# Block-sparse attention and a rational feed-forward layer on one core: turning x by DMA instead of by TensorE, and stores issued by ScalarE

## The chip, the cores and the metric

The kernel runs on one core of a Trainium2 chip. The metric is the device time of one execution in microseconds. Three executions of the kernel before took 824.51, 824.73 and 821.61 us; the median is 824.51 us.

The core has a matrix engine (TensorE, "PE" in the profile, with its weight loads as "PEld"), VectorE ("DVE"), ScalarE ("ACT"), GpSimd ("POOL") and SyncE ("SP"). Each runs its own list of instructions in order. DMAs are issued by one of these engines and then run beside them; a DMA that must wait for a semaphore holds up everything that stands behind it in the list of the engine that issues it.

## The reference

```python
# q, k, v: (4, 8, 768, 64); 24 blocks of 32; 3 sampled key blocks for each query block
scores = scale * np.matmul(q, k.transpose(0, 1, 3, 2))
mask = np.abs(blk_i - blk_j) <= 1
mask = mask | (blk_i == 0) | (blk_j == 0) | (blk_i == n_blocks - 1) | (blk_j == n_blocks - 1)
for qb in range(n_blocks):
    for kb in sampled_blocks[qb]:
        mask[qb * block:(qb + 1) * block, kb * block:(kb + 1) * block] = True
scores = np.where(mask, scores, -1000000000.0)
attn = np.exp(scores - np.max(scores, axis=-1, keepdims=True))
attn = attn / (np.sum(attn, axis=-1, keepdims=True) + 1e-09)
x = np.matmul(attn, v).transpose(0, 2, 1, 3).reshape(3072, 512)

h = x @ w_in                                     # (3072, 2048)
P = a[0] + a[1] * h + a[2] * h * h + a[3] * h * h * h
Q = 1.0 + np.abs(b[0]) * np.abs(h) + np.abs(b[1]) * h * h
out = (P / (Q + 1e-06)) @ w_out                  # (3072, 512)
```

## The kernel before

The 3072 tokens are four batches of 768. A batch has 24 query blocks, worked in pairs (`attention`), and three chunks of 256 tokens, so there are 12 chunks `c` in all. The feed-forward layer runs in units `(c, u)`, eight to a chunk, each with 256 of the 2048 hidden columns (`unit`): the products with w_in into the PSUM tile `ph`, an elementwise chain over ScalarE and VectorE, and the products with w_out into `acc`. A unit needs x of its whole chunk, with features on the partitions, as a high and a low fp16 part (`xh`, `xl`).

Attention makes x with tokens on the partitions: scores from the turned keys `kg` (or `kall`) and queries, row maxima, exponentials, the turning of the probabilities, the products with gathered values `vg` into `av`, and a multiplication by the reciprocal row sum into `xn` (`weigh`, line 983). Four blocks share one `xn`, of which there is one buffer; two such groups make a chunk. A group is then turned by four fp32 transposes on TensorE into one of three shared PSUM banks (`turn_x`, line 995), and two instructions take it out of PSUM, scaled by a power of two, as the high and the low part: `evac_high` on ScalarE (recorded under line 150) and `evac_low` on VectorE (line 1006).

The keys of a batch are turned on TensorE and, for batches 1 to 3, stored to a DRAM scratch `ks` by SP (line 604), from where the key blocks of each part are fetched: a run of four neighbours (line 794), the two edge blocks when a buffer is new to the batch (line 797), and six sampled rows (line 801), whose numbers SP loads into registers (line 717). The pair of the first and the last block of a batch attends to everything and takes three parts of eight blocks (lines 792 and 926). Value blocks come straight from the input (lines 926 to 936) into four `vg` buffers, two for each of a pair's blocks. Output rows are copied from `acc` on ScalarE into an `ld` buffer and stored by SP (line 1159). Nearly all DMAs of the kernel stand in SP's list.

The order of the instructions is made when the kernel is built. Every step is an `Op` with an engine, a price in nanoseconds, its predecessors, a priority and the buffers that it takes; `issue` (line 172) goes through the ops that are ready and always takes the one that can start earliest by these prices, ties by priority. The result is a fixed list for each engine. A price that is a list describes DMAs: each holds the issuing engine for its first number, and the transfer follows. Buffers are tickets of a `Ring`. A pool `ext` opens only when the last weights have been decoded (`switch`, line 1223); it gives four more `ld` buffers and two more key buffers.

Of the kernel before, what the change touches and what calls it, by code (L numbers as in the profile page):

```python
# [24 lines left out]
def kernel(  # L25
# [27 lines left out]
    nc = tc.nc  # L53
# [44 lines left out]
    LAT = {(SC, TE): 410, (VE, TE): 240, (PO, TE): 225, (TE, SC): 200, (TE, VE): 200, (TE, SY): 170, (VE, SC): 130, (VE, PO): 130,  # L98
           (SC, VE): 155, (SC, PO): 180, (PO, VE): 80, (PO, SC): 100}
    OWN = {VE: 127, SC: 143, PO: 96}  # L100
    MARGIN, LATE = 17.0, 1500.0

    class Ring:

# [28 lines left out]
    def row(eng, steps, after, prio, takes=(), uses=()):  # L133

        o, after = None, list(after)
        for n, (price, run) in enumerate(steps):
            o = Op(eng, price, run, [o] if n else after, prio, takes=() if n else takes, uses=list(uses) + (list(takes) if n else []))
        return o
# [144 lines left out]
    r_pr, r_st, r_pT, r_av = Ring([None] * 3), Ring([None] * 4), Ring([None] * PT), Ring(range(2))  # L283
    r_ld, r_kt = Ring([p3] * 3), Ring([p1])
    r_ldq, r_qt, r_fc, r_ks = Ring([None]), Ring([None] * 2), Ring([None] * 2), Ring([None] * 2)
    r_xn = Ring([None])
    r_wl, r_dw, r_kx, r_sums = Ring([None] * 2), Ring([None] * 3), Ring(range(2)), Ring([None] * 2)


# [277 lines left out]
        return p3.tile([P, 2, 2, NS * BLK], F32, name="pr")  # L567

    def new_ld(slot):
        return slot.buf.tile([P, 512], F32, name="ld", bufs=4 if ext and slot.buf is ext[0] else None)  # L570

    def keys(b, t, prio, before, slot, new):


        first, half = b == 0, t % 2
        d = {}
        s_ps = Slot(r_ph if first else r_sp)
        if not first and not half:
            s_kt[b] = Slot(r_kt)
        sks = s_kall if first else [s_kt[b]]  # L580
        sk = sks[0]
        lead = [z for z in sks if not z.left]

        def load():
            d["ld"] = new()
            nc.sync.dma_start(out=d["ld"].rearrange("p (h d) -> p h d", h=H), in_=k[b, :, t * P:(t + 1) * P].rearrange("h p d -> p h d"))

        def transposes():
            d["pt"] = ps_h.tile([P, 512], F32, name="ph") if first else banks[s_ps.buf]
            turned(d["ld"], d["pt"])  # L590

        def evac(eng):
            if first:
                to = kall[:, t * TB:(t + 1) * TB]
            else:
                if not half:
                    kts[b, t // 2] = sk.buf.tile([P, KB, HG, BLK], F32, name="kt") if sk.buf is p1 else sk.buf
                to = kts[b, t // 2][:, half * TB:(half + 1) * TB]
            times(eng, to.rearrange("p b c r -> p c b r"), d["pt"].rearrange("p (c b r) -> p c b r", c=HG, b=TB), 1.0)

        def store():
            if b not in ks_of:
                ks_of[b] = scr.tile([NB, P, HG * BLK], F32, name="ks")
            nc.sync.dma_start(out=ks_of[b][(t // 2) * KB:(t // 2 + 1) * KB].rearrange("b p c -> p b c"), in_=kts[b, t // 2].rearrange("p b c r -> p b (c r)"))

        o_ld = Op(SY, [(475, 262144)], load, () if first else [sc_of[2]], prio - 1, takes=[slot], behind=before)
        o = k_turned[t] = Op(TE, 445, transposes, [o_ld], prio, takes=[s_ps] + lead, uses=[slot])
        o = Op(among("e", VE if first and half else SC, sc=570, ve=610), 0, evac, [o], prio, uses=[s_ps] + sks, behind=k_evac[b][-1] if b in k_evac else None)
        k_evac.setdefault(b, []).append(o)
        if half and not first:  # L610
            k_done[b].append(Op(SY, [(475, 524288)], store, k_evac[b][-2:], prio, uses=[sk, s_scr[b]]))
        return o_ld

    s_kt, sc_of = {}, {}
# [127 lines left out]
    def attention(b, j, prio):  # L742
# [10 lines left out]
        for m, x in enumerate(xs):  # L753
            def one(m, x):
# [30 lines left out]
                else:  # L785
                    s_kg = Slot(r_kg)

                    def load():
                        kg, ks = kgs[s_kg.buf], ks_of[b]
                        flat = kg.rearrange("p s h r -> p s (h r)")  # L790
                        if n > 1:
                            nc.sync.dma_start(out=flat[:, 0:NS], in_=ks[m * NS:(m + 1) * NS].rearrange("b p c -> p b c"))
                            return
                        nc.sync.dma_start(out=flat[:, NR + 2:NR + 6], in_=ks[i - 1:i + 3].rearrange("b p c -> p b c"))
                        if h["new"]:
                            for z in (0, NP - 2):
                                nc.sync.dma_start(out=flat[:, z:z + 2], in_=ks[0:NB:NB - 1].rearrange("b p c -> p b c"))
                        rows = sampled_rows(x)
                        for e in range(2):
                            for r in range(NR):  # L800
                                nc.sync.dma_start(out=flat[:, 2 + e * (NR + 4) + r], in_=ks[bass.ds(rows[e * NR + r], 1)].rearrange("o p c -> p (o c)"))

                    def price():
                        h["new"] = fresh("k", x, s_kg)
# [81 lines left out]
            return 71, lambda: nc.vector.tensor_tensor(out=d["st"][:, 16:20], in0=d["st"][:, 16:20], in1=d["st"][:, 16 + 4 * m:20 + 4 * m], op=ALU.add)  # L886

        def guard():
            nc.vector.tensor_scalar(out=d["st"][:, 28:32], in0=d["st"][:, 16:20], scalar1=1e-9 * 2.0 ** PS_EXP, scalar2=None, op0=ALU.add)

        def invert():
            nc.vector.reciprocal(out=d["st"][:, 32:36], in_=d["st"][:, 28:32])

        oinv = row(VE, [total(m) for m in range(1, n)] + [(70, guard), (81, invert)], oexp[0] + oexp[1], prio[n - 1] + 0.1, uses=[s_st])
        oval = []
        s_av = Slot(r_av)
        for m, x in enumerate(xs):
# [76 lines left out]
            s_xs[c] = Slot(r_xs)  # L974
        w, e4 = (c, e2 // XB), e2 % XB
        if e4 == 0:
            x_group[w] = {"s_xn": Slot(r_xn), "s_ps": Slot(r_sp), "ops": []}
        G = x_group[w]

        def weigh():  # L980
# [2 lines left out]
            nc.vector.tensor_tensor(out=G["xn"][:, e4:e4 + 2].rearrange("p e g d -> p (e g) d"), in0=d["av"].rearrange("p e g d -> p (e g) d"),  # L983
                                    in1=d["st"][:, 32:36].rearrange("p (g o) -> p g o", o=1).broadcast_to([P, 4, D]), op=ALU.mult)

        G["ops"].append(Op(VE, 360, weigh, oval + [oinv], p, takes=[G["s_xn"]] if e4 == 0 else [], uses=[s_av, s_st] + ([G["s_xn"]] if e4 else [])))
        if e4 < XB - 2:
            return
        s_xn, s_ps = G["s_xn"], G["s_ps"]
# [16 lines left out]
            nc.vector.scalar_tensor_tensor(out=x_part(1), in0=G["xt"], scalar=xscales[b], in1=x_part(0), op0=ALU.mult, op1=ALU.subtract)  # L1006

        new = e2 < XB
        a = chain["xt"] = Op(TE, 435, turn_x, G["ops"], p, takes=[s_ps] + ([s_xs[c]] if new else []), uses=[s_xn] + ([] if new else [s_xs[c]]), behind=chain.get("xt"))
        a = chain["ev"] = Op(among("v", SC, sc=520, ve=598), 0, evac_high, [a, v_scale[b]], p, behind=chain.get("ev"), uses=[s_ps, s_xs[c]])  # L1010
        l = Op(VE, 602, evac_low, [a], p, uses=[s_ps, s_xs[c]])
        o_ready.setdefault(c, []).append(l)

    last_near = []
    XB = 4
    x_group = {}


# [17 lines left out]
    def unit(c, u):  # L1036
# [104 lines left out]
        for t in range(CH // P):  # L1141
            def store(t):
# [13 lines left out]
                def write():  # L1156
                    p0 = 0
                    for r0, n in runs(c % NCH * 2 + t):
                        nc.sync.dma_start(out=out[b * S + r0:b * S + r0 + n], in_=e["ob"][p0:p0 + n])
                        p0 += n  # L1160

                if o1:
# [6 lines left out]
                    return  # L1169
                if o1:  # L1170
                    s_ob.left -= 1
                Op(SY, [(475, 262144 // len(runs(c % NCH * 2 + t)))] * len(runs(c % NCH * 2 + t)), write, [a], pk[12], uses=[s_ob])
            store(t)


# [47 lines left out]
    def switch():  # L1223
        early_cm.__exit__(None, None, None)
        ext.append(ctx.enter_context(tc.tile_pool(name="ext", bufs=1)))
        t = max(o.end for o in decoded + last_near)
        r_ld.free += [(t, ext[0])] * 4
        r_kt.free.append((t, kall[:, NP:NP + KB]))
        for j in range(2):
            kgs.append(ext[0].tile([P, NP, HG, BLK], F32, name=f"xkg{j}"))  # L1230
            r_kg.free.append((t, len(kgs) - 1))
# [33 lines left out]
```

## Time and profile before

| | us |
|---|---|
| median of three executions | 824.51 |
| lowest, highest | 821.61, 824.73 |
| the profiled execution | 821.78 |
| its span | 820.0 |
| TensorE busy in it | 776.0 |
| VectorE busy | 668.7 |
| ScalarE busy | 570.6 |
| GpSimd busy | 77.7 |

The span is the time from the first to the last instruction that the profile shows; the execution is 1.8 us longer. Busy time of matmuls is modelled, since they are pipelined, so a busy TensorE need not be at its peak. Waits are put down to what came last by the profile. A row that begins with SPq is SP's queue of DMA issues; what it shows as duration is how long the issue held SP, not the transfer.

### The profile page before, as it was taken

What the parts mean: (1) busy time and instruction counts of PE and PEld (TensorE: products, weight loads), DVE (VectorE), ACT (ScalarE), POOL (GpSimd) and SP (SyncE); (2) the same over time, 40 slices, a digit from 0 to 9 for tenths busy, and PEclk for the clock granted to TensorE, in tenths of its full rate; (3) what the DMA queues carried; (4) which work ended last, traced back from release to release, by engine and by line L of the source; (5) the groups of instructions that cost most, each with busy time, mean ns of one, the idle gap of its engine ahead of it and who ended that gap; (6) DMA issues with size and microseconds to landing.
All of it is one profiled execution on the core that took longest, in us unless ns stands there. A gap on an engine that the chain in (4) does not pass through costs nothing.

```text
span 820.0 us, 26068 instructions
## 1 busy us (share of the span) xinstructions
PE 776.0 (95%) x10227; PEld 551.4 (67%) x10227; DVE 668.7 (82%) x1567; ACT 570.6 (70%) x1263; POOL 77.7 (9%) x128
## 2 busy tenths in 40 slices
PE   7978967789999999999999997999999999999997
PEld 4646655667677766777777766676767767767774
DVE  3868999999988786789788882988887876887886
ACT  2767786966866868776767867676776748767563
POOL 3516442333000000000000000000000000000000
PEclk9999969999999999999999999999999999999999
DMA  8878976546557757646547656546545446320000
GB/s 222 221 215 243 264 196 206 155 116 168 165 150 194 212 139 203 163 138 166 152 135 195 167 154 175 146 125 178 156 132 146 118 125 180 85 65 3 1 26 27
DMA packets 229306, 123.56 MB, mean 151 GB/s; under 512 B 62912, under 2 KB 218944, under 8 KB 229184
## 3 DMA queue, kind: packets, MB, share of 16 engines
q1 hardware_dynamic: 228032, 117.70, 52.2%
q0 software_dynamic: 1152, 4.19, 1.6%
q8 instruction: 81, 1.33, 0.7%
q14 instruction: 41, 0.34, 0.1%
HBM read 110.83 MB, written 11.01 MB: 149 GB/s over the span
## 4 chain that ended last, share of the span: by engine, by line
PE 74%; DVE 13%; DMA 4%; SPq 4%; ACT 3%; issue 2%; ACTq 0%
PE acc L1110 10%; PE ph L1053 9%; PE acc L1116 9%; PE acc L1112 9%; PE ph L1055 9%; PE ph L1054 9%; PE av L957 6%; PE m L834 5%; PE m L911 5%; DMA vg<-in_v_dram 3%; PE m L560 1%; DVE pr L846 1%; PE m L995 1%; DVE tt L1067 1%; DVE dw L455 1%
## 5 line engine op out<-in xcount | busy, mean ns | idle before, releaser
L1053 PE MATMUL ph<-xh,wi 128*128 128x256 f16 x768 | 211.7, 276 | 8.5 <-DVE tt L1070 8.5
L1055 PE MATMUL ph<-xh,wi 128*128 128x256 f16 x768 | 211.5, 275 | 0.0
L1054 PE MATMUL ph<-xl,wi 128*128 128x256 f16 x768 | 211.3, 275 | 0.0
L1060 ACT ACTIVATE sq<-ph,fc 128x512 f32<-128x512 f32 x96 | 65.9, 686 | 106.4 <-PE ph L1055 106.1
L865 ACT ACTIVATE pr<-pr,st 128x256 f32<-128x256 f32 x224 | 110.8, 501 | 16.6 <-DVE st L877 16.6
L1110 PE MATMUL acc<-wo_h,gh 128*128 128x512 f32 x384 | 115.7, 424 | 1.2 <-ACT ld L150 0.7
L1077 DVE SCALAR_TENSOR_TENSOR ab<-sq,absb,ab 128x512 f32<-128x512 f32 x96 | 73.6, 766 | 34.9 <-ACT ab L1074 34.8
L1112 PE MATMUL acc<-wo_l,gh 128*128 128x512 bf16 x384 | 100.8, 385 | 0.0
L1116 PE MATMUL acc<-wo_b,gl 128*128 128x512 bf16 x384 | 98.7, 379 | 1.1 <-DVE gl L1098 1.1
L1053 PEld LDWEIGHTS <-wi 128*128 128x128 f16 x768 | 76.1, 99 | 28.7 <-DVE tt L1070 6.7
L1088 DVE SCALAR_TENSOR_TENSOR gh<-tt,par,rr 128x512 fp32r<-128x512 f32 x96 | 72.9, 761 | 21.9 <-ACT rr L1084 14.1
L846 DVE CUSTOM_DVE_ANT_1 pr<-m,bias 128x256 f32<-128x256 f32 x204 | 76.3, 418 | 13.4 <-PE m L834 13.3
L1054 PEld LDWEIGHTS <-wi 128*128 128x128 f16 x768 | 75.8, 99 | 16.1 <-issue 3.9
L150 ACT ACTIVATE pT<-m 128x512 f32<-128x512 f32 x112 | 64.6, 595 | 26.2 <-PE m L911 24.7
L1055 PEld LDWEIGHTS <-wi 128*128 128x128 f16 x768 | 75.8, 99 | 9.5
L911 PE MATMUL m<-ident,pr 128*128 128x128 f32 x448 | 70.9, 288 | 6.8 <-ACT pT L150 6.1
L1110 PEld LDWEIGHTS acc<-wo_h,gh 128*128 128x128 f32 x384 | 66.8, 192 | 15.2 <-issue 1.6
L1064 ACT ACTIVATE tt<-ph,par,fc 128x512 f32<-128x512 f32 x96 | 74.9, 780 | 0.1
L911 PEld LDWEIGHTS m<-ident,pr 128*128 128x128 f32 x448 | 64.0, 205 | 16.1 <-ACT pT L150 7.1
L1067 DVE TENSOR_TENSOR tt<-tt,sq 128x512 f32<-128x512 f32 x96 | 66.8, 696 | 8.4 <-ACT tt L1064 8.4
L1094 DVE SCALAR_TENSOR_TENSOR tt<-tt,par,ab 128x512 f32<-128x512 f32 x96 | 73.1, 762 | 0.5
L1070 DVE SCALAR_TENSOR_TENSOR tt<-ph,fc,tt 128x512 f32<-128x512 f32 x96 | 71.4, 744 | 0.6
(140 smaller groups left out, 1188.9 us busy)
## 6 DMA issues: line engine op xcount, KB each, us to landing
vg<-in_v_dram SPq DMA_DIRECT2D x312, 64.0 KB, 2.9
vg<-in_v_dram SPq DMA_DIRECT2D x88, 192.0 KB, 3.5
wl<-in_moe_w_out_dram SPq DMA_DIRECT2D x16, 512.0 KB, 4.1
xkg<-ks SPq DMA_DIRECT2D x126, 64.0 KB, 1.9
vg<-in_v_dram SPq DMA_DIRECT2D x12, 512.0 KB, 4.2
xkg<-ks SPq DMA_DIRECT2D x21, 256.0 KB, 3.1
ldq<-in_q_dram SPq DMA_DIRECT2D x20, 256.0 KB, 3.6
out_dram<-ld SPq DMA_DIRECT2D x20, 256.0 KB, 2.8
```

The source lines that it names most:

```text
L846: nc.vector.tensor_tensor_reduce(out=prs[x][:, e, g].rearrange("p (s r) -> p s r", r=BLK), in0=h["sp"][g][:, e], in1=add.rearrange("p (s o ...
L865: nc.scalar.activation(out=prs[x][:, e, g], in_=prs[x][:, e, g], func=AF.Exp, scale=SCALE, bias=st[:, 12 + y:13 + y], accum_out=st[:, 16 + ...
L911: nc.tensor.transpose(pp[:, jj * P:(jj + 1) * P], pr[:, e, g, kt:NS * BLK:2], ident)
L1053: nc.tensor.matmul(o, wh, xh[:, :, cc], start=(cc == 0), stop=False)
L1054: nc.tensor.matmul(o, wh, xl[:, :, cc], start=False, stop=False)
L1055: nc.tensor.matmul(o, wl, xh[:, :, cc], start=False, stop=(cc == NCC - 1))
L1064: nc.scalar.activation(out=d["tt"], in_=d["ph"], func=AF.Identity, scale=d["cst"][:, 3:4], bias=par[:, 2:3])
L1067: nc.vector.tensor_tensor(out=d["tt"], in0=d["tt"], in1=d["sq"], op=ALU.mult)
L1077: nc.vector.scalar_tensor_tensor(out=d["ab"], in0=d["sq"], scalar=absb[:, 1:2], in1=d["ab"], op0=ALU.mult, op1=ALU.add)
L1110: nc.tensor.matmul(acc, g, wo_h[:, f], start=(new and e == 0), stop=False)
L1112: nc.tensor.matmul(acc, g, wo_l[:, f], start=False, stop=False)
L1116: nc.tensor.matmul(acc, g, wo_b[:, f], start=False, stop=(last and e == 1))
```

## The change

From chunk 2 on (`XD = 2`), a group of x is no longer turned on TensorE. The power of two goes into the reciprocal row sum, so that `xn` is already scaled; ScalarE rounds it to fp16 (`split_high`), VectorE forms the rest (`split_low`), both into one SBUF tile `x16`, and two DMA transposes issued by SP put the two halves into `xh` and `xl` (`across`). `x16` has one buffer, in the pool `ext`, which in turn has three `ld` buffers instead of four. The stores of the output and of the turned keys are issued by ScalarE instead of SP, at a price of 400 ns. The scratch for the keys is laid out by partition, so that several neighbouring blocks of a partition lie side by side. The second `weigh` of a group is put behind the first.

```diff
-    MARGIN, LATE = 17.0, 1500.0
+    MARGIN, LATE, QP = 17.0, 1500.0, 400
-    r_xn = Ring([None])
+    r_xn, r_x16 = Ring([None]), Ring([])
-        return slot.buf.tile([P, 512], F32, name="ld", bufs=4 if ext and slot.buf is ext[0] else None)
+        return slot.buf.tile([P, 512], F32, name="ld", bufs=3 if ext and slot.buf is ext[0] else None)
-                ks_of[b] = scr.tile([NB, P, HG * BLK], F32, name="ks")
-            nc.sync.dma_start(out=ks_of[b][(t // 2) * KB:(t // 2 + 1) * KB].rearrange("b p c -> p b c"), in_=kts[b, t // 2].rearrange("p b c r -> p b (c r)"))
+                ks_of[b] = scr.tile([P, NB, HG * BLK], F32, name="ks")
+            nc.scalar.dma_start(out=ks_of[b][:, (t // 2) * KB:(t // 2 + 1) * KB], in_=kts[b, t // 2].rearrange("p b c r -> p b (c r)"))
-            k_done[b].append(Op(SY, [(475, 524288)], store, k_evac[b][-2:], prio, uses=[sk, s_scr[b]]))
+            k_done[b].append(Op(SC, [(QP, 524288)], store, k_evac[b][-2:], prio, uses=[sk, s_scr[b]]))
-                        nc.sync.dma_start(out=flat[:, NR + 2:NR + 6], in_=ks[i - 1:i + 3].rearrange("b p c -> p b c"))
+                        nc.sync.dma_start(out=flat[:, NR + 2:NR + 6], in_=ks[:, i - 1:i + 3])
...
         def guard():
+            if c >= XD:
+                nc.vector.tensor_scalar(out=d["st"][:, 28:32], in0=d["st"][:, 16:20], scalar1=1e-9 * 2.0 ** PS_EXP, scalar2=v_inv[b], op0=ALU.add, op1=ALU.mult)
+            else:
...
-            x_group[w] = {"s_xn": Slot(r_xn), "s_ps": Slot(r_sp), "ops": []}
+            x_group[w] = {"s_xn": Slot(r_xn), "s_ps": Slot(r_x16 if c >= XD else r_sp), "ops": []}
...
+        if c >= XD:
+            def split_high():
+                G["x16"] = ext[0].tile([P, 2, XB * P], F16, name="x16", bufs=1)
+                times(nc.scalar, G["x16"][:, 0], G["xn"].rearrange("p e g d -> p (e g d)"), 1.0)
+
+            def split_low():
+                nc.vector.tensor_tensor(out=G["x16"][:, 1], in0=G["xn"].rearrange("p e g d -> p (e g d)"), in1=G["x16"][:, 0], op=ALU.subtract)
+
+            def across(y):
+                def run():
+                    if c not in xs_of:
+                        xs_of[c] = xbufs[s_xs[c].buf]
+                    nc.sync.dma_start_transpose(out=xs_of[c][y][:, x0:x0 + XB].rearrange("p b c r -> p b (c r)"), in_=G["x16"][:, y])
+                return run
+
+            a = Op(SC, 520, split_high, G["ops"], p, takes=[s_ps], uses=[s_xn])
+            l = Op(VE, 602, split_low, [a], p, uses=[s_ps, s_xn])
+            a = chain["xt"] = Op(SY, [(475, 131072)], across(0), [a], p, takes=[s_xs[c]] if new else [], uses=[s_ps] + ([] if new else [s_xs[c]]), behind=chain.get("xt"))
+            l = chain["xt"] = Op(SY, [(475, 131072)], across(1), [l, a], p, uses=[s_ps, s_xs[c]], behind=chain["xt"])
+            o_ready.setdefault(c, []).extend([a, l])
+            return
-    XB = 4
+    XB, XD = 4, 2
...
-                        nc.sync.dma_start(out=out[b * S + r0:b * S + r0 + n], in_=e["ob"][p0:p0 + n])
+                        nc.scalar.dma_start(out=out[b * S + r0:b * S + r0 + n], in_=e["ob"][p0:p0 + n])
-                Op(SY, [(475, 262144 // len(runs(c % NCH * 2 + t)))] * len(runs(c % NCH * 2 + t)), write, [a], pk[12], uses=[s_ob])
+                Op(SC, [(QP, 262144 // len(runs(c % NCH * 2 + t)))] * len(runs(c % NCH * 2 + t)), write, [a], pk[12], uses=[s_ob])
...
-        r_ld.free += [(t, ext[0])] * 4
+        r_ld.free += [(t, ext[0])] * 3
+        r_x16.free.append((t, None))
```

## Rows read from the trace of the kernel before

**Rows 1.** The page's engines, busy us (share) and instructions.

```profile
PE 776.0 (95%) x10227; PEld 551.4 (67%) x10227; DVE 668.7 (82%) x1567; ACT 570.6 (70%) x1263; POOL 77.7 (9%) x128
```

**Rows 2.** Busy time by stretch: length, PE, PEld, DVE, ACT, POOL, clock, DMA, GB/s.

```profile
348.00:465.00 117.00, 117.00 (x1547) 84.64 (x1546) 98.10 (x232) 83.80 (x183) 0.00 (x0) 1.00 0.59 161
```

**Rows 3.** The page's chain that ended last, shares by engine.

```profile
PE 74%; DVE 13%; DMA 4%; SPq 4%; ACT 3%; issue 2%; ACTq 0%
```

**Rows 4.** Groups of instructions by line and shape: busy us, mean ns, idle before.

```profile
L1067 DVE TENSOR_TENSOR tt<-tt,sq 128x512 f32<-128x512 f32 x96 | 66.8, 696 | 8.4 <-ACT tt L1064 8.4
...
L1006 DVE SCALAR_TENSOR_TENSOR xl<-m,xscale,xh 128x512 f16<-128x512 f32 x24 | 17.8, 746 | 4.7 <-ACT xh L150 4.6
```

**Rows 5.** TensorE's weight loads in order of time, around three of the groups.

```profile
166.28 0.57 PEld L995 LDWEIGHTS m<-ident,xn 128*128 128x128 f32 x4
166.82 0.10 PEld L1053 LDWEIGHTS <-wi 128*128 128x128 f16 x1
...
324.57 0.47 PEld L995 LDWEIGHTS m<-ident,xn 128*128 128x128 f32 x4
...
749.65 0.47 PEld L995 LDWEIGHTS m<-ident,xn 128*128 128x128 f32 x4
750.09 0.10 PEld L1053 LDWEIGHTS <-wi 128*128 128x128 f16 x1
```

**Rows 6.** In order of time: low part ready, first product, of chunks 2 and 11.

```profile
202.09 0.74 DVE L1006 SCALAR_TENSOR_TENSOR xl<-m,xscale,xh 128x512 f16<-128x512 f32 x1
...
226.77 0.27 PE L1053 MATMUL ph<-xh,wi 128*128 128x256 f16 x1
...
751.17 0.74 DVE L1006 SCALAR_TENSOR_TENSOR xl<-m,xscale,xh 128x512 f16<-128x512 f32 x1
...
764.78 0.27 PE L1053 MATMUL ph<-xh,wi 128*128 128x256 f16 x1
```

**Rows 7.** The last weight decoded, on GpSimd, in order of time.

```profile
207.34 1.29 POOL L475 TENSOR_TENSOR wo_l<-dw,wo_h 128x512 bf16<-128x512 f32 x1 [4.04 <-ACT wo_h L150]
```

**Rows 8.** How long an issue holds SP, by line: ns min/median/max, first and last start.

```profile
L1159 SPq DMA_DIRECT2D out_dram<-ld x32: 332/382/1533, 216.8 to 816.5; - x32
L687 SPq DMA_DIRECT2D ldq<-in_q_dram x32: 379/563/1890, 7.8 to 674.4; - x32
```

**Rows 9.** The page's DMA issues: count, KB each, median us from issue to landing.

```profile
ld<-in_v_dram SPq DMA_DIRECT2D x18, 256.0 KB, 4.8
```

**Rows 10.** SP's own waits from 160 to 752 us: total, times, longest.

```profile
SPq L929 <- PE av L957: 49.6, 19, 8.1
...
SPq L929 <- PE acc L1116: 1.3, 1, 1.3
```

**Rows 11.** The chain's longest pieces near 316 and 497 us, then SP's issues before.

```profile
316.41 5.01 DMA vg<-in_v_dram
497.44 3.95 DMA vg<-in_v_dram
302.84 2.61 SPq L801 DMA_DIRECT2D xkg<-ks  x4
...
306.04 0.53 SPq L1159 DMA_DIRECT2D out_dram<-ld  x1
...
315.46 0.38 SPq L1159 DMA_DIRECT2D out_dram<-ld  x1
...
316.41 0.44 SPq L926 DMA_DIRECT2D vg<-in_v_dram  x1
```

**Rows 12.** The end, in order of time: the last copies and stores.

```profile
815.40 1.08 ACT L150 ACTIVATE ld<-acc 128x512 f32<-128x512 f32 x2 [7.32 <-PE acc L1116]
816.02 0.83 SPq L1159 DMA_DIRECT2D out_dram<-ld  x2
```

**Rows 13.** Waits of the engines from 160 to 752 us: total, times, longest.

```profile
ACT sq L1060 <- PE ph L1055: 85.6, 51, 3.9
...
PEld av L957 <- ACT ab L1074: 2.1, 5, 0.4
```

More of the change, by code (lines that the diff above doesn't have):

```diff
@@ L791, in load @@
                         if n > 1:
-                            nc.sync.dma_start(out=flat[:, 0:NS], in_=ks[m * NS:(m + 1) * NS].rearrange("b p c -> p b c"))
+                            nc.sync.dma_start(out=flat[:, 0:NS], in_=ks[:, m * NS:(m + 1) * NS])
                             return
-                        nc.sync.dma_start(out=flat[:, NR + 2:NR + 6], in_=ks[i - 1:i + 3].rearrange("b p c -> p b c"))
+                        nc.sync.dma_start(out=flat[:, NR + 2:NR + 6], in_=ks[:, i - 1:i + 3])
                         if h["new"]:
                             for z in (0, NP - 2):
-                                nc.sync.dma_start(out=flat[:, z:z + 2], in_=ks[0:NB:NB - 1].rearrange("b p c -> p b c"))
+                                nc.sync.dma_start(out=flat[:, z:z + 2], in_=ks[:, 0:NB:NB - 1])
                         rows = sampled_rows(x)
@@ L800, in load @@
                             for r in range(NR):
-                                nc.sync.dma_start(out=flat[:, 2 + e * (NR + 4) + r], in_=ks[bass.ds(rows[e * NR + r], 1)].rearrange("o p c -> p (o c)"))
+                                nc.sync.dma_start(out=flat[:, 2 + e * (NR + 4) + r], in_=ks[:, bass.ds(rows[e * NR + r], 1)].rearrange("p o c -> p (o c)"))
                     def price():
@@ L888, in guard @@
         def guard():
-            nc.vector.tensor_scalar(out=d["st"][:, 28:32], in0=d["st"][:, 16:20], scalar1=1e-9 * 2.0 ** PS_EXP, scalar2=None, op0=ALU.add)
+            if c >= XD:
+                nc.vector.tensor_scalar(out=d["st"][:, 28:32], in0=d["st"][:, 16:20], scalar1=1e-9 * 2.0 ** PS_EXP, scalar2=v_inv[b], op0=ALU.add, op1=ALU.mult)
+            else:
+                nc.vector.tensor_scalar(out=d["st"][:, 28:32], in0=d["st"][:, 16:20], scalar1=1e-9 * 2.0 ** PS_EXP, scalar2=None, op0=ALU.add)
         def invert():
             nc.vector.reciprocal(out=d["st"][:, 32:36], in_=d["st"][:, 28:32])
-        oinv = row(VE, [total(m) for m in range(1, n)] + [(70, guard), (81, invert)], oexp[0] + oexp[1], prio[n - 1] + 0.1, uses=[s_st])
+        oinv = row(VE, [total(m) for m in range(1, n)] + [(70, guard), (81, invert)], oexp[0] + oexp[1] + ([v_scale[b]] if c >= XD else []), prio[n - 1] + 0.1, uses=[s_st])
         oval = []
@@ L984, in weigh @@
                                     in1=d["st"][:, 32:36].rearrange("p (g o) -> p g o", o=1).broadcast_to([P, 4, D]), op=ALU.mult)
-        G["ops"].append(Op(VE, 360, weigh, oval + [oinv], p, takes=[G["s_xn"]] if e4 == 0 else [], uses=[s_av, s_st] + ([G["s_xn"]] if e4 else [])))
+        G["ops"].append(Op(VE, 360, weigh, oval + [oinv], p, takes=[G["s_xn"]] if e4 == 0 else [], uses=[s_av, s_st] + ([G["s_xn"]] if e4 else []),
+                           behind=G["ops"][-1] if e4 else None))
         if e4 < XB - 2:
```

## The prediction

> **What bounds the kernel now.** I read the page's engine shares first: TensorE is busy 95% of the span, and the chain that ended last is TensorE for 74% [rows 1, 3]. A share over the whole span mixes stages, so the busy time by stretch comes next: between 348 and 465 us TensorE has no idle time at all, while VectorE and ScalarE have 16% and 28% to spare [rows 2]. From about 160 us to the last attention part at 750 us, work taken off TensorE should therefore shorten the run nearly one for one, if its inputs keep coming in time. What does hold TensorE up there is mainly two waits for a gathered value tile, 5.01 and 3.95 us [rows 11].
>
> **The PE turning goes.** Chunks 2 to 11 have two groups each, so 20 groups of four fp32 transposes leave TensorE. What one holds is read from the start of its first weight load to the start of the next other weight load: 166.28 to 166.82 us is 0.54, 749.65 to 750.09 us is 0.44 [rows 5]. Over all 20 (these are the first and the last) the median is 0.50 us and the sum 10.2 us. There is nothing to overlap it with, because the neighbours on both sides are matmuls that follow without a gap. **Minus 10.2 us.** The PSUM bank that each group took comes free too; I count nothing for it.
>
> **Split and scale.** High part: ScalarE reads SBUF instead of PSUM, once per group as before. Low part: a VectorE multiply-subtract from PSUM of 0.74 us becomes a subtraction; the nearest row with two SBUF tensors is 0.70 us [rows 4]. 20 times 0.05 us is 1 us on an engine with slack: zero. The scale moves into a second operation of the 128x4 guard instruction: zero. All three are hidden by TensorE's own queue of unit matmuls.
>
> **Later x.** The DMAs put x into place later than an evacuation does. The low part of chunk 2 is ready at 202.8 us and its first product starts at 226.8; for chunk 11 it is 751.9 and 764.8 us, a slack of 12.9 us, the smallest of the ten chunks [rows 6]. Two transfers at the longest median landing of a load on SP, 4.8 us each [rows 9], plus the split, fit into that. Zero from chunk 3 on. Chunk 2 is special: its fp16 pair lives in the space that opens only after the last weight is decoded, at about 208.6 us [rows 7], so its first group, turned at 166 us before, waits for some 42 us, keeps the single xn buffer, and the second group comes behind it. From 208.6 us two rounds of split (1.4 us) and two landings remain: with 2 to 4.8 us a landing the second is in place at 219 to 231 us, against 226.8. Between 0 and 4 us late, once; I take **plus 0.5 us**.
>
> **The transposes on SP.** 40 of them, 128 KB each. Before them a split on ScalarE and VectorE must end, and SP serves in order, so behind a waiting transpose stand the loads of keys, queries and values, and behind those TensorE. No row shows a DMA transpose. The bounds of what one holds SP: below, a plain store of at least 0.33 us; above, the 4.8 us of a whole landing [rows 8, 9]. The nearest kind is the query load, whose pieces are 256 bytes like the 128 fp16 columns of a turned block: median 0.56, longest 1.89 us. Since the turned write is unlike any plain one, I take 1.4 us, in the upper part of that row. Off SP go the stores from 160 us on, 26 of output and 6 of keys, at about 0.4 us each (the output's 0.38 [rows 8], the keys' taken alike), 12.8 us. SP's net gain in work is 56 minus 13, or 43 us. SP's listed waits from 160 to 752 us, added up from the first to the last of the 14 longest, are 142 us [rows 10], so on average it fits three times over. It does not fit where SP waits for nothing: where the three-part attention of a batch's edge blocks meets the loads that prepare the next batch, it issues from 302.84 to 316.41 us and the profile lists no wait for it, and the value load on which TensorE stalls stands at the end of that burst [rows 11]. I count three such bursts, one for each batch after the first; if one group met each, the bill would be 3 times 2.8, or 8.4 us. The groups mostly lie outside (the next one after this burst is turned at 324.57 us [rows 5]), so I take a quarter: **plus 2 us**, with 0 and 8.4 as ends.
>
> [...]
>
> **The stores on ScalarE.** 32 output and 9 key stores, 0.38 us at the median and up to 1.53 us [rows 8]: 16 to 63 us on an engine that from 160 to 752 us waits 85.6 us for the PE's ph alone [rows 13]. They wait for ScalarE's own copies, so the wait is short; behind them stand the activations of the next unit. Each could delay a unit by its 0.38 us, 12 us in all, if ScalarE were late; TensorE's longest listed wait for it in this stretch sums to 2.1 us [rows 13], so I take zero and keep 12 as the upper end. At the very end the last two copies run back to back and SP stores beside them [rows 12]; ScalarE has to do both: **plus 0.4 us**.
>
> **Off SP in the bursts.** Two output stores of 0.5 and 0.38 us lie in the burst ahead of the 5.01 us stall, one at 315.46, 0.95 us before the value load [rows 11]. Keys by partition make the four-row and two-row key loads 128 long pieces instead of 512 or 256 short ones. The value load should come about 1 us earlier in each of the two stalls: **minus 2 us**, between 0 and the whole 9.0. One load buffer less (four to three in the late pool) works against that in the same place, since value loads for the scale share it with the output.
>
> [...]
>
> **Sum.** -10.2 + 0.5 + 2 + 0.4 - 2 = -9.3 us. The profiled execution takes 821.78 us, 1.8 us around its span; it becomes 812.5. It lies 2.7 us under the median of the runs, 824.51, so the median to expect is 824.5 - 9.3, about **815.2 us**.
>
> **The rivals.**
> *The freed time turns into new waits.* The order on every engine is a list made from prices, and all of it is made anew. The 8.4 us of the bursts in full give 821.6, the 12 us of ScalarE's stores in the units 827: about 824 us. For it: a TensorE that is 100% busy has waits hidden in it that appear when it is faster. Against it: VectorE and ScalarE have 16% and more of slack. Chance 0.20.
> *SP becomes the bound (slower than before).* Place: the value loads of the next part, behind two transposes in SP's queue. SP's free time is 142 + 12.8 us over 20 groups, 7.7 us each, so it decides from 3.9 us of SP per transpose. At 4.8 us the excess is 1.9 us a group, 38 us, less the 11.3 of the other terms: about 851 us. Already at 2.5 us the three bursts would take 15 us, giving 828. [...] Chance 0.15, of which most lies between 828 and 835.
> *Both value stalls vanish.* If the new order takes SP's bursts apart, 9.0 us go instead of 2, and SP's extra 2 do not come: -10.2 + 0.5 + 0.4 - 9.0 is -18.3, about 806 us. Chance 0.10.
> *The change does not do what it says*, in that the groups would be turned late and chunk 2 start late with the full 4 us: about 819 us; it stays within the forecast's own range.
>
> **How the numbers follow.** The forecast (808 to 820 us) has a chance of 0.55, the likeliest, so 815.2 is the number. A measurement of this kernel can tell about 0.5% from no change, that is 4.1 us: faster below 820.4, slower above 828.6. Faster: 0.55 + 0.10 = 0.65; same 0.20; slower 0.15. Leaving out the lowest and the highest tenth or so, the range is 805 to 830 us.
>
> **What would show it.** Right: TensorE transposes of xn only for chunks 0 and 1 (16 instructions), no new wait ahead of the first product of a chunk, SP holding each transpose under 2 us, TensorE still without idle time between 348 and 465 us. Wrong: value-tile waits on the chain that grow past 9 us, transposes of 4 us or more on SP, or a late first product of chunk 2.

## The result, and the profile after

The changed kernel takes 832.19 us at the median (829.22 to 833.07), the kernel before beside it 823.63. The ratio is 1.011, with an interval of 1.0083 to 1.0136: slower by 8.6 us, where 815.2 us and a range of 805 to 830 had been forecast.

The page of the changed kernel, its engines and its chain that ended last (the profiled execution takes 832.72 us, its span is 831.0):

```profile
PE 765.7 (92%) x10058; PEld 542.7 (65%) x10147; DVE 665.9 (80%) x1567; ACT 570.7 (69%) x1263; POOL 76.8 (9%) x128
...
PE 65%; DVE 14%; DMA 9%; SPq 5%; issue 3%; ACT 3%; ACTq 0%; POOL 0%; DVEq 0%
```

TensorE is busy 10.3 us less than in [rows 1], and the span is 11.0 us longer. On the chain TensorE fell from 74% to 65%, and DMA rose from 4% to 9% [rows 3]. The freed time, and as much again, has become waiting. By stretch (length, then busy time of PE, PEld, DVE, ACT, POOL, then TensorE's granted clock, DMA share, GB/s):

```profile
348.00:465.00 117.00, 112.61 (x1493) 80.72 (x1511) 94.05 (x229) 80.22 (x179) 0.00 (x0) 0.99 0.56 153
592.00:714.00 122.00, 115.16 (x1555) 82.52 (x1550) 90.45 (x228) 81.00 (x185) 0.00 (x0) 0.97 0.56 149
```

The later stretch in the kernel before:

```profile
592.00:714.00 122.00, 122.00 (x1659) 88.02 (x1657) 96.21 (x235) 87.81 (x198) 0.00 (x0) 1.00 0.48 133
```

TensorE had no idle time in the stretch of [rows 2] nor in this one; now it has 4.4 us and 6.8 us, and a clock that averages 0.99 and 0.97. What the change removes from TensorE did go, and the split is as short as forecast (groups by line: busy us, mean ns, idle before):

```profile
L1019 DVE TENSOR_TENSOR x<-xn,x 128x512 f16<-128x512 f32 x20 | 13.7, 687 | 0.1
...
L999 PE MATMUL m<-ident,xn 128*128 128x128 f32 x16 | 2.6, 277 | 0.2 <-DVE scw L363 0.2
```

How long the new DMAs hold SP (ns min/median/max), and their way to landing in us:

```profile
L1025 SPq DMA_TRANSPOSE xh<-x x20: 1189/1240/3591, 207.6 to 760.3; - x20
L1025 SPq DMA_TRANSPOSE xl<-x x20: 1188/1202/2314, 209.2 to 761.6; - x20
...
DMA to landing us min/median/max: 2.3/2.5/6.0
```

A transpose holds SP 1.2 us at the median (3.6 us at the longest), close to the 1.4 us that the prediction took. So the forecast had the price of one transpose about right. The waits of ScalarE from 160 to 752 us show rows that the kernel before did not have (total, times, longest):

```profile
ACT rr L1109 <- DMA out_dram<-ld: 12.4, 2, 8.8
...
ACT sq L1085 <- DMA out_dram<-ld: 9.6, 2, 5.4
...
ACT rr L1109 <- DMA ldq<-in_q_dram: 8.7, 1, 8.7
ACT rr L1109 <- DMA xkg<-ks: 6.9, 1, 6.9
```

`rr` is a step of a unit's elementwise chain and reads neither queries nor keys nor an output buffer. What it waits behind is a store in ScalarE's list. In order of time, around one such store:

```profile
242.30 0.59 ACT L150 ACTIVATE pT<-m 128x512 f32<-128x512 f32 x1
242.49 1.21 SPq L1025 DMA_TRANSPOSE xl<-x  x1
...
243.78 0.53 SPq L932 DMA_DIRECT2D vg<-in_v_dram  x1
...
244.51 2.19 SPq L939 DMA_DIRECT2D vg<-in_v_dram  x3
...
246.80 1.82 SPq L687 DMA_DIRECT2D ldq<-in_q_dram  x3
...
249.55 1.69 ACTq L1184 DMA_DIRECT2D out_dram<-ld  x2
...
251.57 0.63 ACT L1109 ACTIVATE rr<-rr 128x512 f32<-128x512 f32 x1 [8.68 <-DMA ldq<-in_q_dram]
252.24 0.75 DVE L1113 SCALAR_TENSOR_TENSOR gh<-tt,par,rr 128x512 fp32r<-128x512 f32 x1 [7.14 <-ACT rr L1109]
...
253.98 1.06 PE L1141 MATMUL acc<-wo_b,gl 128*128 128x512 bf16 x4 [2.71 <-DVE gl L1123]
```

ScalarE is done at 242.89 us and reaches the store. It issues it only at 249.55, after a query load that SP issued at 246.80 has landed. The two have nothing to do with each other but a completion semaphore, the counter that the trace shows rising as a transfer lands. Each DMA instruction of this trace carries the number of its semaphore. The 835 DMAs of SP and the 41 of ScalarE share eight of them and take them in one common turn: SP's sequence leaves out 35 turns, which are those of ScalarE's first 35 stores, in their order, and the last six stores follow on SP's last DMA. Not one of the 876 is issued before the transfer that last had the same semaphore has landed. This store and that query load carry the same one; the load lands at 249.47 us. SP's issues did that among themselves already: in the trace of the kernel before, its 836 take the eight in turn without an exception, none ahead of that landing. A store of ScalarE now takes its turn behind a transfer of SP that here was not even issued yet, since two transposes and four value loads stood before it in SP's list. The wait then goes down the unit: `rr` starts after 8.68 us of idle ScalarE, `gh` after 7.14 us of idle VectorE, the products after 2.71 us of idle TensorE. Idle time of ScalarE directly ahead of its stores, added up over the trace, is 33.1 us, in 18 waits (those under 0.3 us left out); in each of the 18 the store starts 0.02 to 0.08 us after the landing of the transfer that last had its semaphore, and all but 1 us of the waits ends with a transfer of SP. The stores' own issues add 16.2 us.

Three of the places where TensorE then stalls, by stretch as above:

```profile
249.00:259.00 10.00, 7.22 (x31) 4.36 (x30) 6.76 (x18) 6.11 (x14) 0.00 (x0) 0.83 0.78 229
382.00:392.00 10.00, 7.45 (x41) 4.98 (x41) 5.11 (x10) 6.48 (x17) 0.00 (x0) 0.83 0.70 208
624.00:638.00 14.00, 9.10 (x49) 6.36 (x48) 5.01 (x11) 7.88 (x19) 0.00 (x0) 0.76 0.58 168
```

In the kernel before TensorE never idled for as long as 0.8 us between 227 and 752 us but at its two value loads [rows 11]. Here it idles 2.8, 2.6 and 4.9 us, 10.2 us together, and its granted clock averages 0.83, 0.83 and 0.76: the profile has the granted clock at 0.50 from 254.9, 388.0 and 630.3 us on, for 3.4, 3.4 and 6.8 us, and at 1.00 in the rest of each stretch. The first two begin 0.9 and 0.4 us after the idle time, the third 2.4 us into it. That is up to half of 13.6 us, 6.8 us, more. Up to 17 us in three places is more than the whole loss against the kernel before.

### The profile page after: what moved, and what is told of

Read it like the earlier page. It is cut to its first block, busy times and chain, and to the rows that moved or that the text cites. A ratio compares the mean times of both kernels' runs of the same rounds, so it can differ in the third digit from the quotient of the medians.

```text
span 831.0 us, 25938 instructions
## 1 busy us (share of the span) xinstructions
PE 765.7 (92%) x10058; PEld 542.7 (65%) x10147; DVE 665.9 (80%) x1567; ACT 570.7 (69%) x1263; POOL 76.8 (9%) x128
## 4 chain that ended last, share of the span: by engine, by line
PE 65%; DVE 14%; DMA 9%; SPq 5%; issue 3%; ACT 3%; ACTq 0%; POOL 0%; DVEq 0%
PE acc L1135 9%; PE ph L1078 8%; PE ph L1079 8%; PE ph L1080 8%; PE acc L1141 8%; PE acc L1137 8%; PE m L834 5%; PE av L960 5%; PE m L914 5%; DMA vg<-in_v_dram 3%; DMA ldq<-in_q_dram 2%; PE m L560 1%; SPq L801 1%; DVE pr L846 1%; DVE ab L1116 1%
## 5 line engine op out<-in xcount | busy, mean ns | idle before, releaser
L1141 PE MATMUL acc<-wo_b,gl 128*128 128x512 bf16 x361 | 94.0, 379 | 7.9 <-DVE gl L1123 3.7
L1137 PE MATMUL acc<-wo_l,gh 128*128 128x512 bf16 x318 | 87.4, 382 | 4.3
L914 PE MATMUL m<-ident,pr 128*128 128x128 f32 x448 | 74.5, 296 | 15.5 <-ACT pr L865 9.0
L914 PEld LDWEIGHTS m<-ident,pr 128*128 128x128 f32 x448 | 64.4, 206 | 27.6 <-ACT pr L865 13.6
L1109 ACT ACTIVATE rr<-rr 128x512 f32<-128x512 f32 x96 | 60.6, 633 | 29.4 <-DMA out_dram<-ld 12.4
L1106 ACT ACTIVATE rr<-ab 128x512 f32<-128x512 f32 x96 | 60.7, 632 | 22.6 <-DVE ab L1102 20.1
```

Of the source, the lines that this page charges most:

```text
L914: nc.tensor.transpose(pp[:, jj * P:(jj + 1) * P], pr[:, e, g, kt:NS * BLK:2], ident)
L1137: nc.tensor.matmul(acc, g, wo_l[:, f], start=False, stop=False)
L1141: nc.tensor.matmul(acc, g, wo_b[:, f], start=False, stop=(last and e == 1))
```

## The experiments

Theory A: ScalarE's stores, which wait for SP's transfers, are the price. Rival B: the transposes hold SP 1.2 us each, and its loads come late. Rival C: the new order of all instructions is worse by itself. Ratios are to the kernel before beside each experiment, with their intervals; 0.1% is 0.8 us.

**The same order, another engine for the stores.** e1 and e2 leave every step of the plan as it is and change only the engine whose list the 41 stores stand in.

```diff
-            nc.scalar.dma_start(out=ks_of[b][:, (t // 2) * KB:(t // 2 + 1) * KB], ...
+            nc.sync.dma_start(out=ks_of[b][:, (t // 2) * KB:(t // 2 + 1) * KB], ...        # e1; e2: nc.gpsimd
-                        nc.scalar.dma_start(out=out[b * S + r0:b * S + r0 + n], ...
+                        nc.sync.dma_start(out=out[b * S + r0:b * S + r0 + n], ...           # e1; e2: nc.gpsimd
```

> The changed kernel with the same order of all instructions, but its 41 stores issued by SP at the same places of the order. Theory A (ScalarE's stores stand behind DMA semaphores that SP's own DMAs hold, 33 us of waits on ScalarE, and TensorE stalls of some 11 us with a slower clock after each): ScalarE's waits go, 812 to 819 us. Theory B (the 40 transposes hold SP 1.2 us each and make its loads late): the stores add work to SP, 830 us or more. Theory C (the new order is worse by itself): 828 to 834 us.

> The same order again, the 41 stores issued by GpSimd, which has no other work after 230 us. Theory A: 810 to 818 us, ScalarE without waits at a store. Theory B: SP has the same load as in the changed kernel, so about 830 us. Theory C: 828 to 834 us.

e1: 821.13 us, ratio 0.9992 (0.9966 to 1.0017), between the ranges of all three theories. e2: 815.55 us, ratio 0.9902 (0.9864 to 0.9941), in the range of theory A. e2 is faster than the kernel before, and its stretches (as above) are full again, but for 0.2 us:

```profile
348.00:465.00 117.00, 117.00 (x1539) 82.87 (x1539) 97.49 (x238) 85.77 (x189) 3.71 (x7) 1.00 0.60 162
...
592.00:714.00 122.00, 121.81 (x1704) 86.44 (x1703) 97.50 (x235) 87.14 (x196) 3.21 (x6) 1.00 0.59 149
```

The same steps as in the timeline above, in e2:

```profile
237.69 0.59 ACT L150 ACTIVATE pT<-m 128x512 f32<-128x512 f32 x1
...
238.11 1.19 POOL L1184 DMA_DIRECT2D out_dram<-ld  x2 [24.33 <-DVE ld L1179]
238.16 0.63 ACT L1109 ACTIVATE rr<-rr 128x512 f32<-128x512 f32 x1
238.22 0.75 DVE L1113 SCALAR_TENSOR_TENSOR gh<-tt,par,rr 128x512 fp32r<-128x512 f32 x1
```

`rr` follows at once where ScalarE had stood idle for 8.68 us. The order of TensorE's weight loads, of VectorE and of SP is the same, row for row, so C alone and B alone both fall: they foresaw 828 us or more here. e1 lies between; SP has the 41 issues again. One place is seen in its waits of TensorE, ahead of the first product of chunk 2, where the changed kernel does not wait:

```profile
PE ph L1078 <- DMA xh<-x: 3.6, 1, 3.6
```

What e2 does not separate: GpSimd's DMAs stand outside the common turn (in the changed kernel's trace the 8 that it issues carry eight other semaphores, and in e2 its idle time ahead of the output stores, 371 us in 13 waits, ends with instructions of ScalarE and VectorE, never with a landing), and nothing of the units stands behind them. SP's waits for its own turns (those of 0.25 us and more, from 160 us on) fall too, from 14.3 to 4.7 us, as a cause or an effect. No run gives ScalarE's stores semaphores of their own, which would be the direct test.

e16 is e2 once more.

> The changed kernel's order with the stores on GpSimd once more: 0.987 to 0.994 of the kernel before, as e2.

818.20 us, ratio 0.9964 (0.9940 to 0.9988), above the range expected. The two intervals just touch: the two measurements of the same kernel put its gain at 0.4% and 1%, and with their intervals at anything from 0.1% to 1.4%. Against the changed kernel's 1.011, GpSimd instead of ScalarE is thus worth 1.5% to 2.1%, 12 to 17 us, and SP instead of ScalarE (e1) 1.2%, 10 us; the profiled spans are 831.0 with ScalarE, 814.2 and 811.3 with GpSimd.

**The issue time without the waits.** e9 takes e2 and lets ScalarE do a copy of 128x128 numbers (0.31 us) at each of the 41 places.

```diff
+                        nc.scalar.activation(out=junk, in_=ident, func=AF.Copy)
                         nc.gpsimd.dma_start(out=out[b * S + r0:b * S + r0 + n], in_=e["ob"][p0:p0 + n])
```

> The changed kernel's order with the stores on GpSimd, and on ScalarE, where each of the 41 stores stood, a copy of 128x128 numbers (about 0.35 us) that nobody reads. Theory A (ScalarE's waits at the stores are the price, not the time that an issue holds it): within 0.4% of the same order without the copies, 0.988 to 0.995 of the kernel before. Rival H (the 0.36 us of each issue delay the units): 1.003 to 1.011.

819.37 us, ratio 0.9954 (0.9928 to 0.998): between e2 and e16, just above the range of theory A and far below that of rival H. The copies hold ScalarE 12.7 us in all, the stores' issues held it 16.2 us. So the time that an issue holds ScalarE costs nothing that can be told here, at most some 4 us against e2. What remains of the 12 to 17 us goes with the waiting.

**ScalarE's stores without the rest of the change.** e3 changes the engine of the stores in the kernel before, planned with 400 ns there.

```diff
-                Op(SY, [(475, 262144 // len(runs(c % NCH * 2 + t)))] * ..., write, [a], pk[12], uses=[s_ob])
+                Op(SC, [(400, 262144 // len(runs(c % NCH * 2 + t)))] * ..., write, [a], pk[12], uses=[s_ob])
```

> The kernel before with one part of the change alone: output and key stores issued by ScalarE, planned at 400 ns. Theory A: ScalarE waits at the stores here too, 830 to 840 us against 824. Theory B and C: nothing to do with it, 822 to 826 us.

827.13 us, ratio 1.0053 (1.0028 to 1.0077): slower, but less than theory A expected and more than B and C did. ScalarE's idle time ahead of stores is 8.6 us here against 33.1. My reading, not tested, is that without transposes SP is closer to its plan, and its transfers are mostly issued by the time ScalarE comes. e3's order is also a new one.

**The transposes alone.** e4 is the kernel before with split and transposes, stores on SP and the old layout of the keys; e7 adds the new layout. Against the changed kernel, both have

```diff
-                        nc.scalar.dma_start(out=out[b * S + r0:b * S + r0 + n], in_=e["ob"][p0:p0 + n])
+                        nc.sync.dma_start(out=out[b * S + r0:b * S + r0 + n], in_=e["ob"][p0:p0 + n])
...
-                Op(SC, [(QP, 262144 // len(runs(c % NCH * 2 + t)))] * ..., write, [a], pk[12], uses=[s_ob])
+                Op(SY, [(475, 262144 // len(runs(c % NCH * 2 + t)))] * ..., write, [a], pk[12], uses=[s_ob])
...
-                ks_of[b] = scr.tile([P, NB, HG * BLK], F32, name="ks")         # e4 alone, with the loads that read it
+                ks_of[b] = scr.tile([NB, P, HG * BLK], F32, name="ks")
```

> The kernel before with the split and the DMA transposes from the third chunk on (and three load buffers in the late pool), stores and the layout of the keys as before. Theory A: the 10.2 us of TensorE come out nearly whole, 812 to 819 us. Theory B: 828 us or more, with value loads late behind the transposes. Theory C: anything between 815 and 834 us.

> Split, transposes and keys by partition, but all stores issued and planned on SP. Theory A: no waits on ScalarE; with the transposes alone at 828 us (old layout of the keys), the new layout gives SP back some time: 819 to 826 us. Theory C (orders differ by chance): anything from 815 to 834 us.

e4: 828.17 us, ratio 1.0087 (1.0055 to 1.012). e7: 825.77 us, ratio 1.0052 (1.0029 to 1.0075). So theory A by itself is wrong too: with no store on ScalarE, 10.2 us less on TensorE still end in a loss (825.77 us lies at the upper end of the range that A gave for e7). Both kernels have the same order, and both have one wait of TensorE for a DMA that the kernel before does not have (from 160 to 752 us):

```profile
PE m L560 <- DMA ldq<-in_q_dram: 6.2, 1, 6.2
```

The query load comes late in SP's queue there, behind transposes, value and key loads and two output stores. But this is not B alone. e1 is e7 in another order: the same instructions, all but a few of the weights' early decoding on the same engines, in the order that was planned for stores on ScalarE. There this wait is missing, and e1 is level with the kernel before (0.9992 against 1.0052 for e7). The order by itself is worth 0.6%, 5 us, here, with half of that either way; so theory C has a share, and the loss of e4 and e7 cannot be put down to SP's load.

**The price of a transpose on SP.** e5 (stores on ScalarE) and e10 (stores on GpSimd) put plain DMAs of the same bytes in the place of the transposes, in the same order. They leave the turning out: x is not turned from chunk 2 on, and the output is not that of the reference. They are there for their times alone.

```diff
-                    nc.sync.dma_start_transpose(out=xs_of[c][y][:, x0:x0 + XB].rearrange("p b c r -> p b (c r)"), in_=G["x16"][:, y])
+                    nc.sync.dma_start(out=xs_of[c][y][:, x0:x0 + XB].rearrange("p b c r -> p (b c r)"), in_=G["x16"][:, y])
```

> The changed kernel in its own order, stores on ScalarE, with each DMA transpose replaced by a plain DMA of the same bytes to the same place (so x is not turned from the third chunk on). Theory A1 (ScalarE's waits arise because SP, held 1.2 us by each transpose where the plan has 0.475, issues late the DMAs on whose semaphores the stores wait): SP is back near the plan, ScalarE's waits at stores fall from 33 us to under 15, 815 to 823 us. Theory A2 (the shared semaphores alone, whatever SP does): 828 to 833 us as the changed kernel.

> The changed kernel's order with the stores on GpSimd and each DMA transpose replaced by a plain DMA of the same bytes (x is not turned from the third chunk on). If the 1.2 us that a transpose holds SP cost TensorE time also where ScalarE is out of the way: 0.982 to 0.987 of the kernel before; if SP has room for them: 0.988 to 0.993 as with the transposes.

e5: 825.27 us, ratio 1.0047 (1.0015 to 1.0078). e10: 809.26 us, ratio 0.9843 (0.9803 to 0.9884). How long one holds SP in e10:

```profile
L1025 SPq DMA_DIRECT2D xh<-x x20: 464/490/2499, 205.1 to 735.1; - x20
L1025 SPq DMA_DIRECT2D xl<-x x20: 465/551/1022, 206.4 to 736.3; - x20
```

0.7 us less for each of 40 DMAs, 28 us of SP, are worth 0.6% (5 us) with the stores on ScalarE and 0.6% to 1.2% (5 to 10 us) with them on GpSimd. That is B's share, each of the three differences with 0.4% to 0.6% either way. In e5 ScalarE's idle time ahead of the stores fell only from 33.1 to 28.3 us, not under 15, and its time lies between the ranges of A1 and A2: my reading that the transposes alone bring the waits about (A1 there) fell.

**x on TensorE, the rest of the change made well.** e11 is the kernel before with keys by partition and stores on GpSimd, in e3's order.

```diff
-                ks_of[b] = scr.tile([NB, P, HG * BLK], F32, name="ks")
+                ks_of[b] = scr.tile([P, NB, HG * BLK], F32, name="ks")
...
-                        nc.sync.dma_start(out=out[b * S + r0:b * S + r0 + n], in_=e["ob"][p0:p0 + n])
+                        nc.gpsimd.dma_start(out=out[b * S + r0:b * S + r0 + n], in_=e["ob"][p0:p0 + n])
```

> The kernel before (x turned on TensorE) with keys by partition and the stores issued by GpSimd, in the order that was planned for ScalarE's stores. If what is left of the change is the 10.2 us of TensorE: 0.996 to 1.003 of the kernel before. If it is SP's relief: 0.988 to 0.993, the same as with the transposes.

824.90 us, ratio 1.0017 (0.9984 to 1.005), no difference. So taking SP's stores away and laying the keys out anew gained nothing in this order. From e11 to e10, which turns nothing on TensorE and pays a plain DMA's price, it is 1.0017 to 0.9843, 1.7%, 14 us with some 4 either way. That is not the turning alone: the orders differ, and TensorE's waits for value tiles, from 160 to 752 us, are 7.4 us in e11 and 1.2 us in e10. What the runs show of the turning by itself is TensorE's busy time, 10.3 us.

**Plans that know more.** e6 plans a transpose with its true 1240 ns; e13 makes the plan count the turns that ScalarE's stores take among SP's transfers, as it always did for SP's own; e14 does both; e8 has the true price and stores planned on GpSimd.

```diff
-                    t = max(t, lanes.pop(0) if e == SY else t) + ns
+                    t = max(t, lanes.pop(0) if e in (SY, SC) else t) + ns
...
-            a = chain["xt"] = Op(SY, [(475, 131072)], across(0), ...
+            a = chain["xt"] = Op(SY, [(1240, 131072)], across(0), ...
```

> The changed kernel planned with 1240 ns for a transpose on SP instead of 475, so the order is made anew. Theory A1: the plan keeps the stores behind what SP has issued, 814 to 824 us. Theory A2: 828 us or more.

> The changed kernel, stores on ScalarE, but the plan makes each of them wait for the DMA eight places before it in the common sequence, as it does for SP's. If the waits come from a plan that does not know this: ScalarE's waits at stores fall from 33 us to under 18, 0.994 to 1.004 of the kernel before. If no plan avoids them: 25 us or more, 1.006 to 1.012.

> As e13, and 1240 ns planned for a transpose instead of 475. If the plan is the cause: waits under 15 us, 0.992 to 1.002. If not: 1.004 or more, like the true price alone (1.007).

> Split, transposes (planned at 1240 ns) and keys by partition, stores issued and planned on GpSimd. Theory A with both causes taken out: 808 to 816 us, the 10.2 us of TensorE whole. Theory C: no better than the same order with GpSimd, 812 to 820 us.

e6: 826.47 us, ratio 1.0073 (1.0036 to 1.011), idle ahead of stores 22.4 us. e13: 830.70 us, ratio 1.0107 (1.0061 to 1.0152), 20.2 us. e14: 826.88 us, ratio 1.0051 (1.0023 to 1.0078), 21.0 us. e8: 818.82 us, ratio 0.9967 (0.9948 to 0.9986), no better than e16, so the 808 to 816 us hoped for did not come. Knowing more lowers the waits by a third and does not bring ScalarE's stores to parity; e13 is as slow as the changed kernel. One reason is in its waits of ScalarE:

```profile
ACT sq L1085 <- DMA out_dram<-ld: 8.5, 2, 4.8
ACT x L150 <- DMA xl<-x: 7.7, 2, 5.7
```

The split waits there for the transposes of the group before to leave the one `x16` buffer. Why its other places are no better is open. Every version that has its stores on ScalarE and x by DMA lies between 1.0047 and 1.011, and every one with GpSimd and x by DMA below 1, so the engine decides more than the plan.

**Further versions with GpSimd.** Both start from e2. e12 moves 12 of the loads for the scales to GpSimd too; e15 turns x by DMA only from chunk 3 on, in an order made anew. Its stores are issued by GpSimd, but, other than its expectation says, still planned on ScalarE.

```diff
-                    nc.sync.dma_start(out=d["ld"], in_=v[b].rearrange(...)[:, j * 512:(j + 1) * 512])                                # e12
+                    (nc.gpsimd if b > 1 else nc.sync).dma_start(out=d["ld"], in_=v[b].rearrange(...)[:, j * 512:(j + 1) * 512])
...
-    XB, XD = 4, 2                                                                                                               # e15
+    XB, XD = 4, 3
```

> The changed kernel's order with the stores on GpSimd, and with them the 12 loads of values for the scales of batches 2 and 3 (256 KB each). If SP's bursts at those loads are what still stalls TensorE (a gap of 4.6 us at 279 us with the stores alone on GpSimd): 0.982 to 0.988 of the kernel before. If not: 0.988 to 0.993.

> Stores issued and planned on GpSimd, split and DMA transposes from the fourth chunk on, chunk 2 turned on TensorE as before. If chunk 2's late x costs some 3 us with its slower clock, and two groups on TensorE cost 1 us: 0.985 to 0.991. If the new order decides: anything from 0.988 to 0.998.

e12: 816.58 us, ratio 0.9921 (0.9897 to 0.9944). e15: 813.32 us, ratio 0.991 (0.9881 to 0.9939). Both beat the kernel before and the changed one. Neither can be told from e2, and e2 and e16, the same kernel, lie as far apart. No gain from moving the 12 loads is seen, and what chunk 2 costs is not resolved by e15. e15, e12 and e2 are the versions to keep.

## Why the prediction was wrong, point by point

- **The PE turning goes, minus 10.2 us: right.** 96 transposes became 16, and TensorE's busy time fell by 10.3 us. (Read again, the weight-load rows of the 20 groups give 10.0 us and a median of 0.44 us, a little under the 10.2 and 0.50 of the prediction; nothing hangs on it.)
- **Split and scale, zero: right.** VectorE's half takes 0.687 us, under the 0.70 us taken; ScalarE's stays one instruction.
- **Later x: right in kind.** A landing takes 2.5 us at the median; no chunk from 3 on waits for x. Chunk 2 did come late, as worked out. The changed kernel's chain has

```profile
225.40 2.32 DMA xl<-x
```

  as the last thing ahead of its second product. TensorE waits 0.8 us there; the 0.5 us taken were a little short, the bound of 4 us holds.
- **The transposes on SP, plus 2 us: mis-sized.** The hold was right (1.2 against 1.4 us). What it costs was counted only where a group meets a burst, a quarter of 8.4 us; e5 and e10 measure 5 to 10 us. SP's average slack, 142 us of waits [rows 10], was the wrong comfort: most of its listed waits are for tiles that TensorE still reads, and work put ahead of the next load shifts that load whether or not SP idled a moment before. That is my reading; the runs show the price, not the way.
- **The stores on ScalarE, zero: the step that failed.** The prediction said that they wait for ScalarE's own copies, so the wait is short, and bounded them by 12 us. They wait for SP's transfers as well: 33.1 us of idle ScalarE ahead of them. Measured: 12 to 17 us against GpSimd, of which the issue time (e9) is 0 to 4, and 10 us against SP. In the kernel before, the chain of this can be seen. Among SP's own waits from 160 to 752 us is

```profile
SPq L929 <- DMA ld<-in_v_dram: 2.4, 1, 2.4
```

  a gathered value load that waits for an `ld` load, which is the same turn-taking within one engine: both carry the same semaphore, the load lands at 504.33 us, and the value load is issued at 504.34. I read those rows as buffers and did not ask which queue the turns belong to. The code says it too: `issue` plans SP's DMAs with eight `lanes`, each free again when its transfer has landed, and has none for ScalarE's. The forecast's check of "who waits behind" was made with ScalarE's idle time [rows 13], which says how long ScalarE has nothing to do, not when: 33 us of waits, placed in the middle of units, met no slack.
- **Off SP in the bursts, minus 2 us: the size came out, the reason did not.** The first stall is still there, and its piece of the chain is longer than the 5.01 us of [rows 11]:

```profile
316.86 6.31 DMA vg<-in_v_dram
```

  The second, at 497 us before, is gone. TensorE's waits for value tiles from 160 to 752 us, before and after:

```profile
PE av L957 <- DMA vg<-in_v_dram: 4.6, 2, 3.5
PE av L960 <- DMA vg<-in_v_dram: 2.6, 1, 2.6
```

  That is the 2 us, but by luck: e11, which takes the stores off SP and lays the keys out anew in another order, has 7.4 us of these waits, not fewer. The order decides here, not SP's relief. (The burst before 316 us was not quite free of waits of SP either, as the prediction has it: the profile lists two, 0.7 us together.)
- **The clock, left out.** The sum priced a stall at its length. In the changed kernel three stalls of 2.6 to 4.9 us each came with 3.4 to 6.8 us at a granted clock of 0.50, up to 6.8 us more in all. No term of the forecast held it.
- **The signs.** Those of a right forecast came in part: 16 transposes are left, and SP is held under 2 us at the median, though 3.6 us once. The one that spoke against it is TensorE's 4.4 us of idle time between 348 and 465 us.
- **The rivals.** "The freed time turns into new waits" gave 824 us and named ScalarE's stores at 12 us. The place was right and the reason was not: its 12 us were the time of the issues, which e9 puts at 0 to 4, and that 12 is also the lower end of what the stores cost is luck. "SP becomes the bound" did not come: a transpose holds SP 1.2 us, below the 3.9 us from which I had let it decide, and e1, in which SP has the transposes and the stores, is level with the kernel before.

Put together from the runs: 1.4 us for e11's own difference, about -14 from e11 to e10 (the turning at a plain DMA's price, and another order), 5 to 10 for the transposes' hold, 12 to 17 for the stores on ScalarE. These are steps of one chain of ratios, from e11 by e10 and e2 or e16 to the changed kernel, so they add up to its 1.1% by construction; the sum confirms none of them.

What stays open: why a plan that counts the turns (e13) is no faster; what of e2's gain is ScalarE's wait itself and what is SP's freer turns; and how much of the differences of 0.5% is the chance of one order against another, which is worth 0.6% between e1 and e7.

## What to carry to other kernels

Before a DMA moves to a compute engine's queue, list what its issue waits for: the data, the buffer, and the completion semaphore whose turn it is, which may belong to a transfer of another queue that is not yet issued (here 33.1 us in 18 waits). An engine with idle time on average may have none to give in the middle of a dependent chain; an engine with nothing queued behind and outside that turn (GpSimd here) made the same stores 12 to 17 us cheaper. And a stall of TensorE like the three here, of 2.6 to 4.9 us, is to be priced with the stretch at a granted clock of 0.50 that came with each of them, 3.4 to 6.8 us long.

## What the hardware showed that had not been expected

A DMA transpose of 128x512 fp16 from SBUF to SBUF holds SP 1.20 to 1.24 us at the median, a plain DMA of the same bytes 0.49 to 0.55 us, yet both land about equally soon after their issue (2.5 and 2.2 us at the median in the changed kernel and e5). Here the price of a transpose is the time that it holds its queue, not the transfer.

In the changed kernel's trace the 835 DMAs issued by SP and the 41 by ScalarE took eight completion semaphores in common turns, and the 8 issued by GpSimd carried eight others. So a store on ScalarE could wait for a load of SP that it has nothing to do with: 33.1 us in 18 waits.
